# Weight conversion shared over three engines, and TensorE's order left to the planner, in a recurrent attention with a PReLU network behind it

## The chip, the cores and the metric

The kernel runs on one core of a Trainium2 chip. A core has a matrix engine (TensorE, PE in the profile, with its weight loads on a row of their own, PEld), three engines for elementwise work (VectorE or DVE, ScalarE or ACT, GpSimd or POOL), a queue engine that issues DMAs (SyncE or SP; ScalarE can issue DMAs too), and two on-chip memories: SBUF, and PSUM, into which TensorE writes. The engines run their own instructions in order and wait for each other by semaphores. The metric is the device time of one execution in microseconds (us), as the median over several runs. A profile is taken of one execution; its span is the time from the first to the last instruction.

## The reference

Input: q, k, v and f_logit of shape (batch 4, heads 8, sequence 768, head dimension 48) in float32, and a network of 384 to 2048 to 384 whose two weight matrices arrive as float64.

```python
f = 1.0 / (1.0 + np.exp(-f_logit))
for t in range(S):
    state = f[:, :, t, :, None] * state + k[:, :, t] (outer) v[:, :, t]
    y[:, :, t] = q[:, :, t] @ state
x = y, heads side by side: (3072 tokens, 384)
h = x @ w_in
g = np.maximum(h, 0.0) + alpha * np.minimum(h, 0.0)
out = g @ w_out
```

Each head so carries a 48 by 48 state through the sequence that every step decays per row and adds to. The network then treats each token alone.

## The kernel before

The work is cut into twelve chunks: six stretches of 128 tokens of the sequence (c), times two pairs of batch elements (bp). A chunk has 2 x 8 heads and 256 tokens. The order is c outside, bp inside. A chunk's state goes on to the chunk of the next c with the same bp.

For each chunk `attention` loads f, q, k and v. Its preparation is work of VectorE, with GpSimd computing running products of the decay (`pre`, `suf`, L203 to L212): products of q and k with decay factors, in `qd`, `kr`, `us`, `k4`, `q3`, `ks`, `kh` (L173 to L233). TensorE then makes these parts: `raw` (L246) and `qu` (L262) for each of the two batch elements, both copied under masks into `ad` by VectorE (L253, L267); `off` (L280); the transposes `pk` (L288), copied by ScalarE to `ksn`; `pd` (L301), which VectorE adds into the state (L314, L315); and `py` (L336, L347), which is the chunk's output. All of these go through the PSUM tag "pair", which has two buffers. ScalarE copies `py` to `y`, and ten small DMAs turn it into `xT` (L358), the network's input.

`network` works through the 2048 hidden columns in eight groups of two blocks of 128: for each block three matmuls (384 rows in three tiles of 128) with the 256 tokens of xT as moving operand, both blocks into one of four PSUM banks, `ph` (L371). The profile counts 96 such records a chunk. ScalarE takes relu(-h) (L376), VectorE combines it with alpha into `g` (L379; the tag has ten buffers, a chunk uses eight). Then, for each of the two batch elements, the sixteen blocks of g are multiplied with w_out into `po` (L386; 64 records a chunk), which ScalarE copies out (L389).

The weights arrive as float64, of which a float32 has to be made by integer and float operations on the two 32-bit halves: `load_weights` does it in 12 pieces of 512 columns for each matrix, and each piece is seven VectorE operations (L134 to L143). Its raw data uses the tag "y", its temporaries the tag "neg".

Which engine does what is in the code. The order of the instructions on an engine is made by a planner when the program is built: it walks through an expected timeline, and gives each engine the first instruction in the order of the program whose inputs and buffers it expects to be ready. For TensorE alone this is switched off before: inside `tc.manual_schedule` (L406) its instructions stay in the order in which the loop at L407 to L424 calls the generators. `attention` and `network` therefore give up control (`yield`) after each stage; the loop puts two, two, one, two and one groups of the previous chunk's ph behind the five stages of the attention, and the previous network's po after the next chunk's preparation. The weights w_in are asked for after chunk 0's attention, w_out after chunk 1's.

Of the kernel before, what the change touches and what calls it, by code (L numbers as in the profile page):

```python
# [14 lines left out]
C = 128  # L15
# [3 lines left out]
U = 2  # L19
# [7 lines left out]
def kernel(  # L27
# [93 lines left out]
    A = const.tile([128, U, H, C], F32, tag="A", name="A")  # L121
    nc.gpsimd.memset(A, 0.0)

    def load_weights(dst, src, name):

        flat = dst.rearrange("p a n -> p (a n)")
        for n in range(0, flat.shape[1], WP):
            raw = work.tile([128, WP, 2], I32, tag="y", name=f"{name}_raw{n}")
            nc.scalar.dma_start(out=raw.rearrange("p n two -> p (n two)"),
                                in_=src[:, n:n + WP].bitcast(I32))  # L130
            lo, hi = raw[:, :, 0], raw[:, :, 1]

            mi = work.tile([128, WP], I32, tag="neg", name=f"{name}_mi{n}", bufs=3)
            nc.vector.tensor_scalar(mi, hi, 0xFFFFF, 0x100000, ALU.bitwise_and, ALU.bitwise_or)  # L134
            m = mi.bitcast(F32)
            nc.vector.scalar_tensor_tensor(m, lo.bitcast(U32), 2.0 ** -32, mi, ALU.mult, ALU.add)

            e = work.tile([128, WP], I32, tag="neg", name=f"{name}_e{n}", bufs=3)
            nc.vector.tensor_scalar(e, hi, 20, 0x7FF, ALU.logical_shift_right, ALU.bitwise_and)
            nc.vector.tensor_scalar(e, e, 1023.0 - 127.0, 0.0, ALU.subtract, ALU.max)  # L140
            nc.vector.tensor_scalar(e, e, 255.0, 2.0 ** 23, ALU.min, ALU.mult)
            nc.vector.scalar_tensor_tensor(e, hi, -0x80000000, e, ALU.bitwise_and, ALU.bitwise_or)
            nc.vector.scalar_tensor_tensor(flat[:, n:n + WP], m, 2.0 ** -20, e.bitcast(F32), ALU.mult, ALU.mult)  # L143

    def rows(par):
        return slice(64 * par, 64 * par + D)
# [2 lines left out]
        return t.rearrange("p (n r) -> p n r", r=4)  # L149

    def attention(bp, c, state, xT):

        i = f"{bp}_{c}"
        b0 = U * bp

        def load(name, src):
            t = work.tile([128, W], F32, tag=name, name=f"{name}_{i}")
            nc.sync.dma_start(out=t.rearrange("p (u x) -> p u x", u=U),
                              in_=src[b0:b0 + U, c].rearrange("u p h t -> p u (h t)"))
            return t  # L160
# [1 line left out]
        f = quads(load("f", fT))  # L162
        nc.scalar.activation(f, f, AF.Sigmoid)
        qdv = [qd[:, d * W:(d + 1) * W] for d in range(4)]
        nc.sync.dma_start(out=qdv[0].rearrange("p (u x) -> p u x", u=U),
                          in_=qT[b0:b0 + U, c].rearrange("u p h t -> p u (h t)"))
        k = load("k", kT)
        vt = work.tile([128, U, DM + 16], F32, tag="v", name=f"v_{i}")
        nc.gpsimd.memset(vt[:, :, DM:DM + 16], 0.0)
# [29 lines left out]
                fq[:, :, 1:1 + n].unsqueeze(3).broadcast_to((128, G, n, 4)), ALU.mult)  # L199


        suf = work.tile([128, G, NB], F32, tag="suf", name=f"suf_{i}")
        nc.gpsimd.memset(suf, 1.0)  # L203
        pin = pre[:, :, 1:NB + 1]
        nc.gpsimd.tensor_copy(pin, fq)
# [8 lines left out]
            h *= 2  # L214


        q3 = work.tile([128, GC, 3, DB], F32, tag="q3", name=f"q3_{i}")
        ks = work.tile([128, GC, 2, DB], F32, tag="ks", name=f"ks_{i}")
        kh = work.tile([128, GC, DB], F32, tag="kh", name=f"kh_{i}")
        for j in range(2):  # L220
            js = slice(j, G, 2)
            nc.vector.tensor_tensor(q3[:, :, 2 * j].rearrange("p g (i r) -> p g i r", r=4), q4[:, js],
# [9 lines left out]
        nc.vector.tensor_tensor(f64.rearrange("p u h c -> p (u h c)").unsqueeze(2),  # L232
                                f32[:, 0:G:2], f32[:, 1:G:2], ALU.mult)  # L233
        qs = q3.rearrange("p (u h c) s t -> p u h c (s t)", h=HP, c=NC2)

        yield


        for u in range(U):
            raw = pair(f"raw{u}_{i}")  # L240
            for hp in range(HP):
                for j in range(NJ):
                    g = (u * HP + hp) * C + j * DB
                    for par in range(2):
                        r_ = rows(par)
                        nc.tensor.matmul(raw[DB * j:DB * (j + 1), par, hp * C:(hp + 1) * C],  # L246
                                         lhsT=k[r_, g:g + DB],
                                         rhs=qd[r_, 0:4 * W].rearrange("p (d x) -> p d x", d=4)[:, :, g:g + DB],
                                         start=True, stop=True)
            adu = ad[:, u].rearrange("p r h t -> p (r h) t")  # L250
            rv = raw.rearrange("p r (h d t) -> p (r h) d t", h=HP, d=4)
            for d in range(4):
                nc.vector.copy_predicated(  # L253
                    adu, mraw[:, d].rearrange("p i r -> p (i r)").bitcast(I32).unsqueeze(1).broadcast_to((128, H, DB)),
                    rv[:, :, d])
            qu = pair(f"qu{u}_{i}")
            for hp in range(HP):
                for j in range(NJ):
                    g = (u * HP + hp) * NJ + j
                    for par in range(2):  # L260
                        r_ = rows(par)
                        nc.tensor.matmul(qu[DB * j:DB * (j + 1), par, hp * UW:(hp + 1) * UW],  # L262
                                         lhsT=k4[r_, g * DB:(g + 1) * DB], rhs=us[r_, g], start=True, stop=True)
            for m in range(1, NB):
                lo = UO[m] + (4 if m == 1 else 0)
                n = DB - 4 * m
                nc.vector.copy_predicated(  # L267
                    ad[:, u, :, :, 4 * m:DB],
                    mquad[:, lo:lo + n].bitcast(I32).unsqueeze(1).unsqueeze(1).broadcast_to((128, 2, HP, n)),
                    qu[:, :, 0:HP * UW].rearrange("p r (h x) -> p r h x", h=HP)[:, :, :, lo:lo + n])  # L270
            yield
        off = pair(f"off_{i}")
        for u in range(U):
            for hp in range(HP):
# [14 lines left out]
        ksn = work.tile([128, U, HP * 128], F32, tag="ksn", name=f"ksn_{i}", bufs=1)  # L289
        for u in range(U):  # L290
            nc.scalar.copy(ksn[:, u], pk[:, u])
        yield
        pd = pair(f"pd_{i}")
        for u in range(U):
            for hp in range(HP):
                for cc in range(NC2):
                    for par in range(2):
# [3 lines left out]
                        nc.tensor.matmul(pd[64 * par:64 * par + 64, cc, o:o + D],  # L301
                                         lhsT=ksn[s_, u, hp * 128 + 64 * par:hp * 128 + 64 * par + 64],
                                         rhs=vt[s_, u, hd * D:(hd + 1) * D], start=True, stop=True)
        states = [state[bp]]
        for cc in range(NC2):
            if c == NC - 1 and cc == NC2 - 1:
                break
            st = work.tile([128, U * HP, D], F32, tag="state", name=f"state{cc}_{i}", bufs=6)
            pdv = pd[:, cc, 0:U * HP * D].rearrange("p (a e) -> p a e", e=D)
            if states[-1] is None:  # L310
                nc.vector.tensor_copy(st, pdv)
            else:
                fv = f64[:, :, :, cc:cc + 1].rearrange("p u h o -> p (u h) o")
                nc.vector.tensor_tensor(st, states[-1], fv.broadcast_to((128, U * HP, D)), ALU.mult)  # L314
                nc.vector.tensor_tensor(st, st, pdv, ALU.add)  # L315
            states.append(st)
        state[bp] = states[-1]
        yield


        for j in range(NJ):
# [17 lines left out]
        for cc in range(NC2):  # L339
            if states[cc] is None:  # L340
                continue
            for u in range(U):
                for hp in range(HP):
                    for par in range(2):
# [2 lines left out]
                        nc.tensor.matmul(py[64 * par:64 * par + D, u, o:o + CH],  # L347
                                         lhsT=states[cc][r_, u * HP + hp], rhs=qs[r_, u, hp, cc, 0:CH],
                                         start=False, stop=True, skip_group_check=True)
        y = work.tile([128, U, HP, C], F32, tag="y", name=f"y_{i}")  # L350
        for u in range(U):
            nc.scalar.copy(y[:, u].rearrange("p h t -> p (h t)"), py[:, u])
        for hd in range(H):
            d = hd * D
            while d < (hd + 1) * D:
                n = min((hd + 1) * D, (d // 128 + 1) * 128) - d
                p0 = 64 * (hd % 2) + d - hd * D
                nc.sync.dma_start(  # L358
                    out=xT[d % 128:d % 128 + n, d // 128].rearrange("p (u t) -> p u t", u=U),
                    in_=y[p0:p0 + n, :, hd // 2])  # L360
                d += n
        yield

    def network(bp, c, xT):
        i = f"{bp}_{c}"
        gs = []
        for f in range(0, NF, 2):
# [11 lines left out]
                nc.vector.scalar_tensor_tensor(g[:, j], neg[:, j], om[:, f + j:f + j + 1], phv[:, j],  # L379
                                               ALU.mult, ALU.add)  # L380
            gs.append(g)
            yield
        for u in range(U):
            po = bank(f"po{u}_{i}")
            for f in range(NF):
                nc.tensor.matmul(po[:, 0:DM], lhsT=gs[f // 2][:, f % 2, u * C:(u + 1) * C], rhs=w_out_sb[:, f],  # L386
                                 start=(f == 0), stop=(f == NF - 1))
            o = work.tile([128, DM], F32, tag="o", name=f"o{u}_{i}", bufs=3)
            nc.scalar.copy(o, po[:, 0:DM])  # L389
            t0 = ((U * bp + u) * NC + c) * C  # L390
            nc.sync.dma_start(out=out[t0:t0 + C], in_=o)
        yield

    steps = [(bp, c) for c in range(NC) for bp in range(B // U)]
    state = [None] * (B // U)

    def begin(n):
        x = work.tile([128, NK, T], F32, tag="xT", name=f"xT_{n}")  # L400
        a = attention(*steps[n], state, x)
        next(a)
        return a, x

    att = net = None
    with tc.manual_schedule(engines={mybir.EngineType.PE}):  # L406
        for n in range(len(steps) + 1):  # L407
            if n == 0:
                att, x = begin(n)
            for stage in range(5):  # L410
                if n < len(steps):
                    next(att)
                for _ in range((2, 2, 1, 2, 1)[stage]):
                    if net is not None:
                        next(net)
            if n < 2:
                load_weights((w_in_sb, w_out_sb)[n], (w_in, w_out)[n], ("w_in", "w_out")[n])
            if n < len(steps):
                last = network(*steps[n], x)
            if n + 1 < len(steps):  # L420
                att, x = begin(n + 1)
            if net is not None:
                next(net)
            net = last  # L424


# [53 lines left out]
```

## Time and profile before

| | |
|---|---|
| Runs | 781.1, 782.22 and 784.5 us; median 782.22 |
| The profiled execution | 781.1 us, span 779.2 us |
| TensorE busy | 658.2 us (84% of the span) |
| VectorE busy | 435.6 us (56%) |
| ScalarE busy | 159.1 us (20%) |
| GpSimd busy | 70.6 us (9%) |
| DMA traffic | 46.79 MB, mean 60 GB/s |
| Mean granted TensorE clock | 0.936 |

Busy time counts instructions in execution; the rest of the span an engine waits. A line "L371 PE MATMUL ph<-xT,w_in_sb" names the source line, the engine, the operation, what is written and what is read. Behind it stand the count, the busy time, the mean of one in ns, and the idle time just before these instructions with what ended it. The tenths are the busy share in each of 40 equal slices of the span. Not all idle time costs something: only that of the engine which sets the end at that moment.

### The profile page before, as it was taken

How to read it: one execution, taken by the hardware profiler on the slowest of the kernel's cores; microseconds unless marked ns; L12 is line 12 of the kernel's file. 1: busy time of each engine (PE TensorE's matmuls, PEld its weight loads, DVE VectorE, ACT ScalarE, POOL GpSimd, SP SyncE). 2: the span in 40 equal slices, each digit the busy share in tenths (PEclk: the TensorE clock that was granted, in tenths of full speed). 3: DMA queues.
4: the chain of work that ended last, by engine and by line, in shares of the span. 5: the costliest groups of instructions: out<-in, count | busy, mean ns of one | idle time of the engine just before them, and what ended most of it. 6: DMA issues, size and time to landing. Idle time of an engine off the chain costs nothing.

```text
span 779.2 us, 17567 instructions
## 1 busy us (share of the span) xinstructions
PE 658.2 (84%) x7712; PEld 485.5 (62%) x7712; DVE 435.6 (56%) x920; ACT 159.1 (20%) x289; POOL 70.6 (9%) x228
## 2 busy tenths in 40 slices
PE   0350186468999999899999999999999999999998
PEld 0350175124876777777867857768778678587684
DVE  5798997892861842933916808618439157052030
ACT  2030023000330411410411403204104114041110
POOL 8212002000020020020020100200200200000000
PEclk9995589557999999999999999999999999999999
DMA  4224432440220210211212202202101110000000
GB/s 177 83 84 122 159 105 76 135 145 26 69 67 21 84 42 22 83 41 28 80 48 66 56 24 70 65 22 83 41 23 55 51 40 8 24 13 22 21 0 21
DMA packets 31468, 46.79 MB, mean 60 GB/s; under 512 B 3744, under 2 KB 19104, under 8 KB 31392
## 3 DMA queue, kind: packets, MB, share of 16 engines
q1 hardware_dynamic: 27648, 33.04, 14.2%
q10 hardware_dynamic: 3744, 12.63, 5.1%
q8 instruction: 61, 1.00, 0.5%
q14 instruction: 15, 0.12, 0.1%
HBM read 36.22 MB, written 4.72 MB: 53 GB/s over the span
## 4 chain that ended last, share of the span: by engine, by line
PE 67%; DVE 21%; DMA 5%; POOL 3%; ACT 1%; issue 1%; SPq 1%; ACTq 0%; DVEq 0%; POOLq 0%
PE po L386 31%; PE ph L371 24%; PE py L336 3%; DVE qd L182 3%; PE py L347 3%; DVE g L379 2%; DVE ad L267 2%; PE raw L246 2%; DMA qd<-in_qT 2%; DVE ad L253 2%; PE pd L301 2%; PE pk L288 2%; PE qu L262 1%; DMA w_in_raw<-in_w_in 1%; DMA w_out_raw<-in_w_out 1%; DVE k L191 1%
## 5 line engine op out<-in xcount | busy, mean ns | idle before, releaser
L371 PE MATMUL ph<-xT,w_in_sb 128*128 128x256 f32 x1152 | 269.2, 390 | 37.5 <-DVE w_in_sb L143 37.5
L386 PE MATMUL po<-w_out_sb,g 128*128 128x384 f32 x768 | 264.5, 504 | 29.3 <-DVE w_out_sb L143 29.3
L371 PEld LDWEIGHTS ph<-xT,w_in_sb 128*128 128x128 f32 x1152 | 218.4, 194 | 73.0 <-DVE w_in_sb L143 39.2
L386 PEld LDWEIGHTS po<-w_out_sb,g 128*128 128x128 f32 x768 | 149.0, 196 | 140.5 <-DVE w_out_sb L143 32.9
L253 DVE COPY_PREDICATED ad<-mraw,raw 128x256 f32<-128x256 int32 x96 | 42.7, 444 | 174.6 <-PE raw L246 172.4
L379 DVE SCALAR_TENSOR_TENSOR g<-neg,om,ph 128x256 f32<-128x256 f32 x192 | 84.3, 475 | 72.5 <-ACT neg L376 72.2
L376 ACT ACTIVATE neg<-ph 128x512 f32<-128x512 f32 x96 | 57.3, 597 | 201.6 <-PE ph L371 131.8
L389 ACT COPY o<-po 128x384 f32<-128x384 f32 x24 | 11.5, 478 | 278.5 <-PE po L386 278.5
L267 DVE COPY_PREDICATED ad<-mquad,qu 128x224 f32<-128x224 int32 (+6 forms) x168 | 49.7, 296 | 5.2 <-DVE ad L253 0.5
L246 PE MATMUL raw<-qd,k 48*32 48x128 f32 x1536 | 29.4, 286 | 19.4 <-DVE qd L182 19.4
L196 DVE TENSOR_TENSOR us<-us,fq 128x768 f32<-128x768 f32 (+2 forms) x72 | 44.3, 615 | 0.0
L203 POOL MEMSET suf<- 128x256 f32 x12 | 3.7, 311 | 418.4 <-DVE ks L225 418.4
L246 PEld LDWEIGHTS raw<-qd,k 48*32 48x32 f32 x1536 | 22.8, 110 | 28.5 <-POOL pre L212 19.4
L262 PE MATMUL qu<-us,k 48*32 48x116 f32 x1536 | 27.3, 273 | 12.4 <-DVE us L196 6.9
L323 ACT COPY A<-ad 32x512 f32<-32x512 f32 x48 | 29.6, 617 | 20.1 <-DVE ad L267 19.7
L262 PEld LDWEIGHTS qu<-us,k 48*32 48x32 f32 x1536 | 22.5, 109 | 13.7 <-DVE us L196 7.3
L232 DVE TENSOR_TENSOR f<-pre 128x16 f32<-128x16 f32 x12 | 2.2, 184 | 47.8 <-POOL pre L212 47.7
L210 POOL TENSOR_TENSOR suf<-suf,pre 128x32 f32<-128x32 f32 (+2 forms) x84 | 28.8, 368 | 1.8
L182 DVE TENSOR_TENSOR qd<-qd,f 128x768 f32<-128x768 f32 (+2 forms) x36 | 27.5, 764 | 1.9 <-DMA qd<-in_qT 1.8
L336 PE MATMUL py<-A,v 128*64 128x128 f32 x384 | 24.9, 285 | 2.5 <-DVE us L196 2.5
L288 PE MATMUL pk<-ident,ks 128*128 128x128 f32 x96 | 13.9, 291 | 14.5 <-DVE ad L267 11.7
L336 PEld LDWEIGHTS py<-A,v 128*64 128x64 f32 x384 | 22.0, 143 | 6.3 <-issue 6.3
(60 smaller groups left out, 429.8 us busy)
## 6 DMA issues: line engine op xcount, KB each, us to landing
f<-in_fT SPq DMA_DIRECT2D x12, 512.0 KB, 3.7
k<-in_kT SPq DMA_DIRECT2D x12, 512.0 KB, 5.5
qd<-in_qT SPq DMA_DIRECT2D x12, 512.0 KB, 4.0
w_in_raw<-in_w_in ACTq DMA_DIRECT2D x12, 512.0 KB, 3.5
w_out_raw<-in_w_out ACTq DMA_DIRECT2D x12, 512.0 KB, 3.5
v<-in_v SPq DMA_DIRECT2D x12, 384.0 KB, 3.3
out<-o SPq DMA_DIRECT2D x24, 192.0 KB, 1.9
xT<-y SPq DMA_DIRECT2D x72, 48.0 KB, 2.0
```

What stands on the lines that cost most here:

```text
L182: nc.vector.tensor_tensor(quads(qdv[d])[:, :, d:4], quads(qdv[d - 1])[:, :, d:4], f[:, :, 1:5 - d], ALU.mult)
L196: nc.vector.tensor_tensor(us[:, :, UO[m]:UO[m] + 4 * n].rearrange("p g (i r) -> p g i r", r=4), us[:, :, skip:skip + 4 * n].rearrange("p g ...
L246: nc.tensor.matmul(raw[DB * j:DB * (j + 1), par, hp * C:(hp + 1) * C], lhsT=k[r_, g:g + DB], rhs=qd[r_, 0:4 * W].rearrange("p (d x) -> p d ...
L253: nc.vector.copy_predicated(adu, mraw[:, d].rearrange("p i r -> p (i r)").bitcast(I32).unsqueeze(1).broadcast_to((128, H, DB)), rv[:, :, d])
L262: nc.tensor.matmul(qu[DB * j:DB * (j + 1), par, hp * UW:(hp + 1) * UW], lhsT=k4[r_, g * DB:(g + 1) * DB], rhs=us[r_, g], start=True, stop= ...
L267: nc.vector.copy_predicated(ad[:, u, :, :, 4 * m:DB], mquad[:, lo:lo + n].bitcast(I32).unsqueeze(1).unsqueeze(1).broadcast_to((128, 2, HP, ...
L323: nc.scalar.copy(A[s_, :, :, s_], ad[s_].rearrange("p u r h t -> p u (r h) t"))
L336: nc.tensor.matmul(py[64 * par:64 * par + 64, u, hp * C:(hp + 1) * C], lhsT=vt[:, u, hd * D:hd * D + 64], rhs=A[:, u, par * HP + hp], star ...
L371: nc.tensor.matmul(ph[:, j * T:(j + 1) * T], lhsT=w_in_sb[:, kt, (f + j) * 128:(f + j + 1) * 128], rhs=xT[:, kt], start=(kt == 0), stop=(k ...
L376: nc.scalar.activation(neg, phv, AF.Relu, scale=-1.0)
L379: nc.vector.scalar_tensor_tensor(g[:, j], neg[:, j], om[:, f + j:f + j + 1], phv[:, j], ALU.mult, ALU.add)
L386: nc.tensor.matmul(po[:, 0:DM], lhsT=gs[f // 2][:, f % 2, u * C:(u + 1) * C], rhs=w_out_sb[:, f], start=(f == 0), stop=(f == NF - 1))
```

## The change

The conversion of a piece has four VectorE operations in place of seven; two steps are done by ScalarE (`activation` with Relu, which scales and shifts the exponent field and cuts it off at zero, and with Copy, which scales the mantissa) and the last product by GpSimd. The raw tiles have a tag of their own with four buffers and are loaded by SP's queue; the temporaries use the tag "g". The pieces of w_in come in the order in which the network's tiles need them: for each block of 512 columns, the three row blocks.

TensorE's order is no longer fixed: `manual_schedule`, the generators and the loop with stages are gone. A plain loop calls the attention of a chunk, the weights' load in the first two, and then the network of the chunk before, and the planner orders TensorE's instructions like those of the other engines.

To make room, several tags go from two buffers to one (`suf`, `q3`, `ks`, `kh`, `y`), the state's from six to five, `o` from three to two. q is loaded into a tile of its own and copied by ScalarE to `qd`, instead of by DMA straight to `qd`. The ten DMAs from y to xT are split between the queues of SP and ScalarE.

```diff
+    bias = const.tile([128, 1], F32, tag="bias", name="bias")
+    nc.gpsimd.memset(bias, -896.0 * 2.0 ** 23)
...
-        for n in range(0, flat.shape[1], WP):
-            raw = work.tile([128, WP, 2], I32, tag="y", name=f"{name}_raw{n}")
-            nc.scalar.dma_start(out=raw.rearrange("p n two -> p (n two)"),
-                                in_=src[:, n:n + WP].bitcast(I32))
+        ks = NK if dst is w_in_sb else 1
+        per = flat.shape[1] // ks
+        for n in [k * per + j for j in range(0, per, WP) for k in range(ks)]:
+            raw = work.tile([128, WP, 2], I32, tag="raw", name=f"{name}_raw{n}", bufs=4)
+            nc.sync.dma_start(out=raw.rearrange("p n two -> p (n two)"),
+                              in_=src[:, n:n + WP].bitcast(I32))
             lo, hi = raw[:, :, 0], raw[:, :, 1]
 
-            mi = work.tile([128, WP], I32, tag="neg", name=f"{name}_mi{n}", bufs=3)
+            e = work.tile([128, WP], I32, tag="g", name=f"{name}_e{n}", bufs=10)
+            nc.vector.tensor_scalar(e, hi, 0x7FF00000, None, ALU.bitwise_and)
+            nc.scalar.activation(e, e, AF.Relu, bias=bias, scale=8.0)
+
+            mi = work.tile([128, WP], I32, tag="g", name=f"{name}_mi{n}", bufs=10)
             nc.vector.tensor_scalar(mi, hi, 0xFFFFF, 0x100000, ALU.bitwise_and, ALU.bitwise_or)
             m = mi.bitcast(F32)
-            nc.vector.scalar_tensor_tensor(m, lo.bitcast(U32), 2.0 ** -32, mi, ALU.mult, ALU.add)
-
-            e = work.tile([128, WP], I32, tag="neg", name=f"{name}_e{n}", bufs=3)
-            nc.vector.tensor_scalar(e, hi, 20, 0x7FF, ALU.logical_shift_right, ALU.bitwise_and)
-            nc.vector.tensor_scalar(e, e, 1023.0 - 127.0, 0.0, ALU.subtract, ALU.max)
-            nc.vector.tensor_scalar(e, e, 255.0, 2.0 ** 23, ALU.min, ALU.mult)
+            nc.scalar.activation(m, mi, AF.Copy, scale=2.0 ** -20)
+            nc.vector.scalar_tensor_tensor(m, lo.bitcast(U32), 2.0 ** -52, m, ALU.mult, ALU.add)
             nc.vector.scalar_tensor_tensor(e, hi, -0x80000000, e, ALU.bitwise_and, ALU.bitwise_or)
-            nc.vector.scalar_tensor_tensor(flat[:, n:n + WP], m, 2.0 ** -20, e.bitcast(F32), ALU.mult, ALU.mult)
+            nc.gpsimd.tensor_tensor(flat[:, n:n + WP], m, e.bitcast(F32), ALU.mult)
...
-        nc.sync.dma_start(out=qdv[0].rearrange("p (u x) -> p u x", u=U),
-                          in_=qT[b0:b0 + U, c].rearrange("u p h t -> p u (h t)"))
+        q = load("q", qT, 1)
+        nc.scalar.copy(qdv[0], q)
...
-                nc.sync.dma_start(
+                (nc.sync if hd % 2 else nc.scalar).dma_start(
...
-    with tc.manual_schedule(engines={mybir.EngineType.PE}):
-        for n in range(len(steps) + 1):
-            if n == 0:
-                att, x = begin(n)
-            for stage in range(5):
-                if n < len(steps):
-                    next(att)
-                for _ in range((2, 2, 1, 2, 1)[stage]):
-                    if net is not None:
-                        next(net)
-            if n < 2:
-                load_weights((w_in_sb, w_out_sb)[n], (w_in, w_out)[n], ("w_in", "w_out")[n])
...
+    for c in range(NC):
+        for bp in range(B // U):
+            xT = work.tile([128, NK, T], F32, tag="xT", name=f"xT_{bp}_{c}")
+            state[bp] = attention(bp, c, state[bp], xT)
+            if c == 0:
+                load_weights((w_in_sb, w_out_sb)[bp], (w_in, w_out)[bp], ("w_in", "w_out")[bp])
+            if todo is not None:
+                network(*todo)
+            todo = (bp, c, xT)
+    network(*todo)
```

More of the change, by code (lines that the diff above doesn't have):

```diff
@@ L154, in attention, with load @@
         b0 = U * bp
-        def load(name, src):
-            t = work.tile([128, W], F32, tag=name, name=f"{name}_{i}")
+        def load(name, src, bufs=2):
+            t = work.tile([128, W], F32, tag=name, name=f"{name}_{i}", bufs=bufs)
             nc.sync.dma_start(out=t.rearrange("p (u x) -> p u x", u=U),
@@ L199, in attention @@
                 fq[:, :, 1:1 + n].unsqueeze(3).broadcast_to((128, G, n, 4)), ALU.mult)
-        suf = work.tile([128, G, NB], F32, tag="suf", name=f"suf_{i}")
+        suf = work.tile([128, G, NB], F32, tag="suf", name=f"suf_{i}", bufs=1)
         nc.gpsimd.memset(suf, 1.0)
@@ L214, in attention @@
             h *= 2
-        q3 = work.tile([128, GC, 3, DB], F32, tag="q3", name=f"q3_{i}")
-        ks = work.tile([128, GC, 2, DB], F32, tag="ks", name=f"ks_{i}")
-        kh = work.tile([128, GC, DB], F32, tag="kh", name=f"kh_{i}")
+        q3 = work.tile([128, GC, 3, DB], F32, tag="q3", name=f"q3_{i}", bufs=1)
+        ks = work.tile([128, GC, 2, DB], F32, tag="ks", name=f"ks_{i}", bufs=1)
+        kh = work.tile([128, GC, DB], F32, tag="kh", name=f"kh_{i}", bufs=1)
         for j in range(2):
@@ L234, in attention @@
         qs = q3.rearrange("p (u h c) s t -> p u h c (s t)", h=HP, c=NC2)
-        yield
         for u in range(U):
@@ L270, in attention @@
                     qu[:, :, 0:HP * UW].rearrange("p r (h x) -> p r h x", h=HP)[:, :, :, lo:lo + n])
-            yield
         off = pair(f"off_{i}")
@@ L291, in attention @@
             nc.scalar.copy(ksn[:, u], pk[:, u])
-        yield
         pd = pair(f"pd_{i}")
@@ L303, in attention @@
                                          rhs=vt[s_, u, hd * D:(hd + 1) * D], start=True, stop=True)
-        states = [state[bp]]
+        states = [state]
         for cc in range(NC2):
@@ L307, in attention @@
                 break
-            st = work.tile([128, U * HP, D], F32, tag="state", name=f"state{cc}_{i}", bufs=6)
+            st = work.tile([128, U * HP, D], F32, tag="state", name=f"state{cc}_{i}", bufs=5)
             pdv = pd[:, cc, 0:U * HP * D].rearrange("p (a e) -> p a e", e=D)
@@ L316, in attention @@
             states.append(st)
-        state[bp] = states[-1]
-        yield
         for j in range(NJ):
@@ L349, in attention @@
                                          start=False, stop=True, skip_group_check=True)
-        y = work.tile([128, U, HP, C], F32, tag="y", name=f"y_{i}")
+        y = work.tile([128, U, HP, C], F32, tag="y", name=f"y_{i}", bufs=1)
         for u in range(U):
@@ L361, in attention @@
                 d += n
-        yield
+        return states[-1]
     def network(bp, c, xT):
@@ L381, in network @@
             gs.append(g)
-            yield
         for u in range(U):
@@ L387, in network @@
                                  start=(f == 0), stop=(f == NF - 1))
-            o = work.tile([128, DM], F32, tag="o", name=f"o{u}_{i}", bufs=3)
+            o = work.tile([128, DM], F32, tag="o", name=f"o{u}_{i}")
             nc.scalar.copy(o, po[:, 0:DM])
@@ L391, in network @@
             nc.sync.dma_start(out=out[t0:t0 + C], in_=o)
-        yield
-    steps = [(bp, c) for c in range(NC) for bp in range(B // U)]
+    todo = None
     state = [None] * (B // U)
[L399 to L405, printed above, removed]
-    with tc.manual_schedule(engines={mybir.EngineType.PE}):
-        for n in range(len(steps) + 1):
-            if n == 0:
-                att, x = begin(n)
-            for stage in range(5):
-                if n < len(steps):
-                    next(att)
-                for _ in range((2, 2, 1, 2, 1)[stage]):
-                    if net is not None:
-                        next(net)
-            if n < 2:
-                load_weights((w_in_sb, w_out_sb)[n], (w_in, w_out)[n], ("w_in", "w_out")[n])
[L418 to L424, printed above, removed]
+    for c in range(NC):
[8 more added lines that the diff above has]
+    network(*todo)
 def _level_masks():
```

## The prediction

> **What bounds the kernel now.** I read the page's busy shares and slices first, then a table of stretches, then the groups, the chain of waits and the timeline.
>
> The page, busy share and then tenths in 40 slices of 19.5 us:
>
> ```profile
> PE 658.2 (84%) x7712; PEld 485.5 (62%) x7712; DVE 435.6 (56%) x920; ACT 159.1 (20%) x289; POOL 70.6 (9%) x228
> ...
> PE   0350186468999999899999999999999999999998
> ...
> DVE  5798997892861842933916808618439157052030
> ```
>
> TensorE is full from the eleventh slice on and half empty before; VectorE is the reverse. Two kernels in one: a start of some 185 us that VectorE sets, and the rest, which TensorE sets. The stretches say how sharply (columns: length, then busy us and instructions of PE, PEld, DVE, ACT, POOL, then granted clock, DMA share, GB/s):
>
> ```profile
> 60.00:80.00 20.00, 1.22 (x2) 0.50 (x2) 16.77 (x39) 0.00 (x0) 3.03 (x6) 0.50 0.45 138
> 80.00:100.00 20.00, 5.60 (x13) 4.06 (x14) 19.45 (x40) 0.00 (x0) 0.00 (x0) 0.51 0.46 139
> ...
> 160.00:180.00 20.00, 12.40 (x16) 4.29 (x16) 19.35 (x40) 0.00 (x0) 0.00 (x0) 0.50 0.41 129
> ...
> 400.00:450.00 50.00, 48.95 (x639) 37.30 (x638) 28.43 (x61) 13.13 (x24) 4.80 (x17) 1.00 0.19 54
> ```
>
> At 60 to 100 and 140 to 180 us VectorE does conversion and ScalarE nothing; PE has two to sixteen matmuls in 20 us, at half clock. The waits name the cause, and the only one that recurs later (total, times, longest):
>
> ```profile
> PE ph L371 <- DVE w_in_sb L143: 37.5, 3, 17.2
> ...
> PE po L386 <- DVE w_out_sb L143: 29.3, 12, 9.0
> ...
> PE pk L288 <- DVE ad L267: 11.7, 9, 2.4
> ```
>
> The steady part, from the chain in order of time: po groups begin at 338.95, 392.62, 446.27, 500.07, so a chunk takes 53.7. Its pure TensorE work: the last network, alone, 20.72 (ph) + 20.66 (po) = 41.4; attention by start-to-start times at 302.9 to 336.1: raw and qu 2 x 1.9, off 0.8, pk 1.0, pd 1.1, py 3.8 = 10.5. Sum 51.9, so TensorE waits 1.8 a chunk. From 185.05, where PE runs without gaps, the span closes as: rest of the first po 9.5 + ten chunks 537 + 3 (one chunk was 56.6) + last network 41.4 + 3.3 after PE's end = 594; 185 + 594 = 779.
>
> **What the Trainium skill says.** "TensorE: Matmul & The Clock Gate", section "What's actually happening": an idle TensorE is gated to half its clock. The trace agrees: 0.50 in the conversion stretches, 1.00 once full, so every gap closed also speeds what follows it. "SBUF — State Buffer", "Who interferes with whom": a VectorE operation with two SBUF inputs, or in its two-port mode, and a GpSimd operation that reads SBUF exclude each other. The trace agrees in part:
>
> ```profile
> 12.98 2.30 POOL L210 TENSOR_TENSOR suf<-suf,pre 128x32 f32<-128x32 f32 x4
> ...
> 336.98 1.09 POOL L210 TENSOR_TENSOR suf<-suf,pre 128x32 f32<-128x32 f32 x4
> ```
>
> The same four operations take 2.30 beside a working VectorE and 1.09 beside an idle one, while VectorE's L182 grew only from 0.96 to 1.15.
>
> **The change, part by part.** The rows used:
>
> ```profile
> L136 DVE SCALAR_TENSOR_TENSOR w_out_mi<-w_out_raw,w_out_mi 128x512 f32<-128x512 uint32 x12 | 8.2, 685 | 0.0
> ...
> L139 DVE TENSOR_SCALAR w_out_e<-w_out_raw 128x512 int32<-128x512 int32 x12 | 5.1, 422 | 0.0
> ...
> L376 ACT ACTIVATE neg<-ph 128x512 f32<-128x512 f32 x96 | 57.3, 597 | 201.6 <-PE ph L371 131.8 <-DVE w_in_sb L143 48.3 <-issue 19.3
> ```
>
> *VectorE.* A piece now has four TENSOR_SCALAR at about 0.43 and three SCALAR_TENSOR_TENSOR at 0.69: 3.78, 24 pieces 90.7. After: 2 x 0.43 + 2 x 0.69 = 2.24, 53.7. Saved 37.0, all on the engine that sets the start.
>
> *GpSimd* gets one 128x512 product a piece. Not in the trace. L210 and L212 take 0.27 at 32 columns and 0.45 at 128, 1.85 ns a column, so 1.16 us; the skill's "GPSIMD Engine Reference", "3.1 Elementwise — side-by-side cycle accounting", has 2.6 cycles per element, 4497 ns at 2048, a quarter of which is 1.12. 24 x 1.16 = 28 us beside some 110 us: GpSimd has room. What it takes from VectorE through the shared port lies between 0 and 28; I take 10, since in the trace GpSimd bore most of the wait.
>
> *ScalarE* gets two operations a piece from SBUF: L163 takes 1.06 at 1024, so about 0.63 at 512, and the skill's "ScalarE: Activation LUTs", "What ACT_TABLE_LOAD costs", adds 93 ns for the bias column: 24 x 1.35 = 32, and the q copy 12 x 1.06 = 13. ScalarE is 20% busy and idle in the conversion stretches: nothing, if pieces overlap. Without that cover a piece is a relay of VectorE, ScalarE, VectorE and GpSimd of some 5 us; with four raw buffers, up to five pairs of g buffers and attention work to fill in, the relay is hidden.
>
> *Loads.* Weights move from ScalarE's queue, where the first waited until 53.45 for the y buffer, to SP with four buffers of their own, so they can start at once: 12.6 MB at q10's rate (12.63 MB in 5.1% of 779 = 40 us) is hidden under VectorE. Each of 24 issues waits, with the raw buffer, for VectorE's last use; behind it on SP stand loads of f, q, k, v and half the xT stores, late by up to one piece, 2.2, covered by VectorE's queue in the start. Ten xT stores a chunk took 6.4 on SP; split over two queues about 3, and the others cost ScalarE some 3 us of issue a chunk. Covered later by network matmuls; uncovered 2 to 3 a chunk. The q buffer lets q load early and replaces DMA waits by a 1.06 copy.
>
> *Single buffers* for suf, q3, ks, kh, y: the six operations at L222 to L230 (6 x 0.68 = 4.1) must wait until the previous chunk's off, pk or py is done. The 20 us of po matmuls hide that; uncovered 4.1 a chunk.
>
> *Order of pieces.* The first network can start after 3 pieces of w_in instead of 9. Now its first ph groups stalled till 95.6; afterwards they can run from when xT lands, about 57.
>
> *End of the start.* VectorE's work before the last w_out piece: attention (435.6 - 90.7 conversion - 84.3 at L379 - 2.8 for om) / 12 = 21.5 a chunk. Two chunks 43.0 + conversion 53.7 + half a network's L379 3.5 + port 10 = 110.2. At 90% busy (93% in 40 to 120 us now, less for the relay) 122, from 9.3 on: 132 instead of 181. The third chunk's preparation, some 16 us of VectorE work that now stands ahead of w_out, comes after it in program order.
>
> *TensorE's order.* Without the fixed order the planner places PE's instructions as it does the other engines': the first in the program among those it expects to be ready. That is attention n ahead of network n-1, which fills its holes. How good are its expectations? In the timeline VectorE's order, which it made, puts 2.5 us of other work between the state sum at 328.65, which follows pd, and the g pair at 331.19, which follows twelve ph matmuls (2.6 us) and a 0.6 activation; more ready work was at hand (L229) and was put behind. So it expected about the real PE time. It expected GpSimd faster than it is: VectorE waited 4.76 at L232, ahead of a g that was ready. So PE's order should be usable, but each of some eight hand-offs a chunk (raw, qu, raw, qu, off, pk, pd, py) is placed as soon as expected. I take 0.3 late at each, 2.4 a chunk, for today's 1.8, of which pk's wait (11.7 over nine) may go: 2.5. Bounds: 1, and 7.
>
> *Sum.* At 132, PE has left: half the first ph 10.4, its po 20.7, ten chunks at 51.9 + 2.5 = 544, last network 41.4, tail 3.3: 620. Span 752. The profiled execution took 781.1 for a span of 779.2; with those 1.9, 754, and the median of the runs lies 1.1 above that execution: **755 us**, against 782.22.
>
> **The rivals.**
> 1. *Slower: the fixed order was worth more than the start.* Place: attention's hand-offs in the ten full chunks. At 0.9 late each, 7.0 a chunk: 132 + 595 + 70 = 797, run 800. It decides from 5.2 a chunk. For: a chunk's slack above PE's work is only 1.8, bought by 5 us of ph matmuls placed by hand at every hand-off, and GpSimd is misjudged. Against: 20 us of po matmuls are free to fill.
> 2. *Port-bound conversion:* the whole 28 lands on VectorE, 18 more at 90%: end of the start 152, run 775. For: nearly all conversion operations read two inputs or use two ports. Against: L182's small growth.
> 3. *Better:* no port loss, the relay full, 1.8 a chunk: (100.2 / 0.97) + 9.3 = 113; 113 + 594 + 3 = 730 by run.
> 4. *It doesn't do what it says:* the planner holds the first network behind attention until VectorE is through, and start and order cancel: 782. For: L379 stands after w_out in program order. Against: VectorE's 37 us alone move the end of w_out's conversion forward.
>
> **How the numbers follow.** Likeliest 0.50, own range 738 to 768; better 0.12; port-bound 0.10; cancelled 0.05; slower 0.23. Some 0.5% is about what a measurement of this kernel can tell from no change. Faster 0.72, same 0.05, slower 0.23. The range, 728 to 802, leaves about 0.05 below and 0.12 above.
>
> **What would show it.** Right: in the slices VectorE full and PE low until about 130 us, then full; conversion groups at 2 x 0.43 and 2 x 0.69 on VectorE; GpSimd's products at 1.2 to 2; po groups 54 to 55 apart. Wrong: VectorE idle in the start behind ScalarE, GpSimd or a raw load (relay or port); PE waits of several us a chunk on L253, L267 or L323's line (rival 1), or raw matmuls split up among ph, which would lengthen the attention's 10.5.

## The result, and the profile after

The changed kernel takes 792.93 us (792.04 to 793.55, four runs) against 782.67 for the kernel before: ratio 1.0129, 95% interval 1.0104 to 1.0155. It is slower by 1.3%, where 755 us and faster was forecast. The profiled execution has a span of 790.0 us.

The page after, busy share and tenths in 40 slices (19.75 us each):

```profile
PE 660.0 (84%) x7712; PEld 490.1 (62%) x7712; DVE 413.5 (52%) x848; ACT 199.3 (25%) x349; POOL 124.1 (16%) x253
...
PE   0255551999989998989989989989989979989998
...
DVE  6799897937257257167076076086085094043030
```

TensorE is full three slices earlier than before, as forecast, but then has an 8 in every third slice where it had nines. The table of stretches (length, then PE, PEld, DVE, ACT, POOL busy us and instructions, clock, DMA share, GB/s) gives both ends:

```profile
120.00:140.00 20.00, 5.21 (x72) 4.18 (x73) 14.28 (x26) 6.66 (x11) 17.44 (x19) 0.50 0.21 64
140.00:160.00 20.00, 20.00 (x77) 14.38 (x76) 16.97 (x34) 3.81 (x6) 4.28 (x13) 1.00 0.09 27
...
400.00:450.00 50.00, 45.69 (x573) 34.69 (x557) 28.90 (x63) 13.66 (x24) 4.82 (x17) 1.00 0.18 57
```

In the steady part PE has 45.7 busy us in 50, before 48.95, both at a granted clock of 1.00: what is lost there is time in which TensorE stands, not clock. The chain in order of time (start, length, what) shows the same as a period, before:

```profile
181.17 13.71 PE po L386 x36
...
446.27 20.64 PE po L386 x64
...
500.07 20.64 PE po L386 x64
```

and after:

```profile
148.95 20.64 PE po L386 x64
...
204.68 20.64 PE po L386 x64
...
320.52 20.64 PE po L386 x64
...
378.40 20.64 PE po L386 x64
```

From one chunk's po to the next it is 57.9 us, before 53.7. The two effects work against each other. The first network's po ends at 169.6 instead of 194.9: 25 us gained. From there to the end the ten chunks cost 36 us more. The difference is the 11 us between the spans.

Where the steady 57.9 goes is in the timeline of one chunk (start, length, engine, line, what; in brackets the idle time before it and what ended it):

```profile
341.98 1.07 PE L267 MATMUL qu<-us,k 48*32 48x116 f32 x64
342.30 1.89 DVE L258 COPY_PREDICATED ad<-mraw,raw 128x256 f32<-128x256 int32 x4 [20.19 <-PE raw L251]
...
344.33 1.15 PE L251 MATMUL raw<-qd,k 48*32 48x128 f32 x64 [1.28 <-DVE ad L258]
...
345.41 0.70 PE L372 MATMUL ph<-xT,w_in_sb 128*128 128x256 f32 x2
...
346.76 1.08 PE L267 MATMUL qu<-us,k 48*32 48x116 f32 x64 [0.66 <-DVE ad L272]
...
349.73 0.75 PE L284 MATMUL off<-q,kh 48*32 48x32 f32 x64 [0.39 <-DVE ad L258]
...
355.43 1.15 PE L304 MATMUL pd<-v,ksn 64*64 64x48 f32 x64 [1.20 <-ACT ksn L295]
...
359.56 1.97 PE L337 MATMUL py<-A,v 128*64 128x128 f32 x32 [0.62 <-ACT A L324]
```

The second raw stands right behind the first qu. It needs the PSUM buffer that VectorE's four masked copies are still reading, and TensorE waits 1.28 us. Before, 24 ph matmuls (5.4 us) stood there:

```profile
303.77 1.08 PE L262 MATMUL qu<-us,k 48*32 48x116 f32 x64
...
304.78 5.45 PE L371 MATMUL ph<-xT,w_in_sb 128*128 128x256 f32 x24
...
310.15 1.16 PE L246 MATMUL raw<-qd,k 48*32 48x128 f32 x64
```

Now two ph records, then six, six, six and ten stand between the attention's groups, and 66 behind them, where the only wait is 0.27. With that 0.27 the waits of this chunk are 4.4 us. The rest of the 5.9 above the 51.9 of pure work is in the changes between the attention's small matmuls and ph: two ph records take 0.70 where they take 0.43 in a row, and the seven stretches of ph of this chunk come to 1.5 more than 96 records in a row. The ends of matmuls are modelled in the profile, so the split between wait and change is less sure than their sum.

### The profile page after: what moved, and what is told of

Read it like the earlier page. It is cut to its first block, busy times and chain, and to the rows that moved or that the text cites. A ratio compares the mean times of both kernels' runs of the same rounds, so it can differ in the third digit from the quotient of the medians.

```text
span 790.0 us, 17642 instructions
## 1 busy us (share of the span) xinstructions
PE 660.0 (84%) x7712; PEld 490.1 (62%) x7712; DVE 413.5 (52%) x848; ACT 199.3 (25%) x349; POOL 124.1 (16%) x253
## 4 chain that ended last, share of the span: by engine, by line
PE 49%; DVE 29%; POOL 8%; ACT 5%; DMA 4%; issue 3%; ACTq 1%; SPq 0%; POOLq 0%; DVEq 0%
PE po L386 31%; PE ph L372 14%; DVE ad L258 5%; DVE ad L272 4%; DMA f<-in_fT 3%; POOL suf L217 3%; POOL pre L219 3%; ACT A L324 3%; DVE us L194 2%; POOL pre L212 2%; DVE g L380 2%; DVE qd L189 2%; DVE q L229 2%; DVE us L203 1%; PE py L337 1%
## 5 line engine op out<-in xcount | busy, mean ns | idle before, releaser
L386 PE MATMUL po<-w_out_sb,g 128*128 128x384 f32 x768 | 249.6, 486 | 0.0
L372 PEld LDWEIGHTS ph<-xT,w_in_sb 128*128 128x128 f32 x1152 | 216.7, 193 | 52.6 <-issue 22.4
L386 PEld LDWEIGHTS po<-w_out_sb,g 128*128 128x128 f32 x768 | 145.9, 190 | 99.2
L380 DVE SCALAR_TENSOR_TENSOR g<-neg,om,ph 128x256 f32<-128x256 f32 x192 | 81.8, 475 | 97.1 <-ACT neg L377 91.2
L251 PE MATMUL raw<-qd,k 48*32 48x128 f32 x1536 | 31.8, 302 | 50.5 <-DVE qd L189 35.4
L251 PEld LDWEIGHTS raw<-qd,k 48*32 48x32 f32 x1536 | 24.7, 116 | 58.9 <-issue 37.9
L176 POOL MEMSET v<- 128x32 f32 x12 | 1.8, 148 | 368.3 <-PE py L337 368.3
L267 PE MATMUL qu<-us,k 48*32 48x116 f32 x1536 | 29.2, 285 | 30.5 <-DVE ad L272 13.4
L328 ACT COPY A<-off 32x256 f32<-32x256 f32 x48 | 15.1, 360 | 47.0 <-PE off L284 46.8
L219 POOL TENSOR_TENSOR pre<-pre 128x32 f32<-128x32 f32 (+2 forms) x84 | 26.5, 342 | 0.9
```

The costliest lines, as they stand in the source:

```text
L372: nc.tensor.matmul(ph[:, j * T:(j + 1) * T], lhsT=w_in_sb[:, kt, (f + j) * 128:(f + j + 1) * 128], rhs=xT[:, kt], start=(kt == 0), stop=(k ...
```

## Experiments

Theory H: the loss is TensorE's order, with the attention's groups placed one close behind the other. Its rivals: the planner as such; the single buffers, q copy and stores that lengthen the attention's own chain; a conversion that gained nothing. "Period" below is the time from one chunk's po to the next, as most settled chunks have it; single chunks are up to 3.8 us longer. Ratios are to runs of the kernel before made beside each run (medians 782.4 to 783.2).

### The order put back, in two ways

`conv_fixed` is the changed kernel with the stages, the loop and the fixed order of before. `conv_staged` has the stages and the loop, but not the fixed order, so its diff is the same without the `manual_schedule` line. The loop over `n` is that of before, and so are the places of the `yield`s:

```diff
-    todo = None
...
+    steps = [(bp, c) for c in range(NC) for bp in range(B // U)]
...
+    with tc.manual_schedule(engines={mybir.EngineType.PE}):
+        for n in range(len(steps) + 1):
...
```

> The changed kernel, with TensorE's order of before put back (stages, loop and fixed order); conversion, loads, single buffers, q copy and split xT stores stay as changed. Theory H (the loss is TensorE's order: attention groups placed one behind the other, with too few ph matmuls between them, 5.9 us of waits and switches a chunk in place of 1.8): po groups again about 53.7 apart, the earlier end of the start kept, so 782.7 - 25 = about 757 us (750 to 765). Rival S (the single buffers, the q copy and the stores on ScalarE make the attention's own chain longer): 57 to 58 apart in this order too, 790 to 800 us.

> As conv_fixed, with the stages and the loop that sets ph groups behind them in the program, but TensorE left to the planner. Theory H1 (what costs is the plain loop's order of calls, which the planner takes as priority): the steady order is nearly the fixed one, period 53.5 to 54.5, 750 to 765 us. Rival H2 (the planner's expectations themselves are too short, so any order of its own loses): period above 56, 775 us or more.

Measured: `conv_staged` 759.5 us, ratio to before 0.9693 (0.9665 to 0.9721), period mostly 55.2. `conv_fixed` 801.82 us, ratio 1.0233 (1.0198 to 1.0268), period 55.6 to 57.3. H1 gets the time right, with the period 0.7 above its range; for `conv_fixed` I had expected 757 and missed by 45.

More than half of that miss is in the start: the second po begins at 230.7, where 25 us ahead of the 227.9 of before would be 203. The rest is the period; all of TensorE's waits from 250 to 650 us are at pk (20.9 us). TensorE's waits over the whole run in `conv_fixed` (total, times, longest):

```profile
PE pk L295 <- DVE ad L274: 30.5, 10, 3.7
PE po L393 <- POOL w_out_sb L151: 30.4, 12, 8.9
```

and the timeline of TensorE there (columns as above):

```profile
152.14 1.65 PE L393 MATMUL po<-w_out_sb,g 128*128 128x384 f32 x2 [2.98 <-POOL w_out_sb L151]
156.03 2.93 PE L393 MATMUL po<-w_out_sb,g 128*128 128x384 f32 x4 [2.24 <-POOL w_out_sb L151]
159.92 1.65 PE L393 MATMUL po<-w_out_sb,g 128*128 128x384 f32 x2 [0.96 <-POOL w_out_sb L151]
```

A piece of w_out arrives every 3.89 us: the relay of VectorE, ScalarE, VectorE and GpSimd runs one piece at a time. VectorE's first operation of a piece waits for GpSimd's product (in the changed kernel this line has no wait):

```profile
L142 DVE TENSOR_SCALAR w_out_e<-w_out_raw 128x512 int32<-128x512 int32 x12 | 5.1, 427 | 15.1 <-POOL w_out_sb L151 15.1
```

In the fixed order all of the first network's ph precedes po, so when w_out is converted its eight g tiles can hold eight of the tag's ten buffers; a piece needs two. That this is the reason is read from the code; the wait above agrees with it, but no run with more buffers was made. The prediction had named "up to five pairs of g buffers" as the relay's cover; here the cover was gone, and the seven VectorE operations of before, at 3.8, would have been no slower. The first po ends at 194.1, in the kernel before at 194.9.

### Each part alone

`before_plain` is the kernel before with only the plain loop (no stages, no fixed order). `order_only` is the kernel before with its stages and loop, and TensorE left to the planner (the `manual_schedule` line taken out). `planner_old_conv` is the changed kernel with the old conversion (its seven VectorE operations, and its loads on ScalarE's queue):

```diff
-        for n in [k * per + j for j in range(0, per, WP) for k in range(ks)]:
+        for n in range(0, flat.shape[1], WP):
...
```

> The kernel before with the plain loop of the changed kernel and TensorE left to the planner; conversion, loads, buffers and q as before. The one part alone. Theory H1 (the plain loop costs what the steady part loses): po groups 57 to 58 apart, 10 x 3.8 more than before, less what the planner gains in the start (order_only: 19 us): 798 to 812 us. Rival (single buffers, q copy and stores are needed for the loss): 54 to 55 apart, below 775 us.

> The kernel before with the planner ordering TensorE too, the staged loop kept; nothing else changed. Theory H1 (what costs in the changed kernel is the plain loop's order of calls, not the planner): po groups 53.5 to 54.5 apart as in before (54.0), and the start a little shorter, since PE no longer stands behind a ph that waits for weights: 765 to 780 us. Rival H2 (the planner loses by itself): over 56 apart, 795 or more.

> The changed kernel with the seven-operation conversion of before (loads on ScalarE's queue, matrices in row order, raw tiles in their own tag with four buffers); plain loop and planner stay. Theory H: period 57.8 as in the changed kernel, and the start ends later by the conversion's worth, 793 + 25 = 812 to 825 us. Rival C (the conversion gained little, the earlier end of the start came from the plain loop's order): 793 to 800 us.

| kernel | us | ratio to before (interval) | period | second network's po begins at |
|---|---|---|---|---|
| before | 782.7 | 1 | 53.7 | 227.9 |
| order_only | 763.55 | 0.9767 (0.9733 to 0.9802) | 53.7 | 212.5 |
| before_plain | 829.36 | 1.0599 (1.0556 to 1.0642) | 57.1 | 240.8 |
| planner_old_conv | 809.15 | 1.033 (1.0299 to 1.0362) | 57.8 | 222.9 |
| changed | 792.93 | 1.0129 (1.0104 to 1.0155) | 57.9 | 204.7 |
| conv_staged | 759.5 | 0.9693 (0.9665 to 0.9721) | 55.2 | 194.4 |

In the staged program the planner is acquitted: it keeps the period at 53.7 and begins sooner, since TensorE stands for less time at ph and po that lack their weights (35.5 us instead of 66.8 over the whole run). With the plain loop as well the period is 57.1 and the kernel 6% slower than before, more than the 798 to 812 I had expected, because its start got longer too: one qu waited 28.9 us, until 184.5, for the end of w_out's conversion on VectorE. The plain loop in a fixed order was not run. The new conversion with its loads and order of pieces is worth 16 us with the same plain loop (809.15 to 792.93; theory H had put it at 19 or more), all ahead of the second po (222.9 to 204.7).

### The product on GpSimd

```diff
-            nc.gpsimd.tensor_tensor(flat[:, n:n + WP], m, e.bitcast(F32), ALU.mult)
+            nc.vector.tensor_tensor(flat[:, n:n + WP], m, e.bitcast(F32), ALU.mult)
```

> The changed kernel with the last product of a piece on VectorE in place of GpSimd (five VectorE operations). Theory P (GpSimd's product costs VectorE through the shared port about what it saves: conversion took 71.8 us of VectorE time instead of 53.7): each of the four other operations back to 0.43 and 0.69, conversion 53.7 + 24 x 0.69 = 70 us, time the same within 4 us (789 to 797). Rival (the stretch is not GpSimd's doing): conversion 88 us on VectorE, the start longer by 15 to 20, 808 or more.

Measured: 789.93 us, ratio to before 1.0084 (1.0053 to 1.0115). Groups of w_out in the changed kernel (count, busy us, mean ns of one, idle before):

```profile
L151 POOL TENSOR_TENSOR w_out_sb<-w_out_mi,w_out_e 128x512 f32<-128x512 f32 x12 | 18.2, 1537 | 16.7 <-DVE w_out_mi L149 15.2 <-DVE w_out_e L150 1.5
...
L149 DVE SCALAR_TENSOR_TENSOR w_out_mi<-w_out_raw,w_out_mi 128x512 f32<-128x512 uint32 x12 | 10.2, 861 | 0.0
```

and in this one:

```profile
L149 DVE SCALAR_TENSOR_TENSOR w_out_mi<-w_out_raw,w_out_mi 128x512 f32<-128x512 uint32 x12 | 8.2, 686 | 0.6 <-ACT w_out_mi L148 0.6
...
L151 DVE TENSOR_TENSOR w_out_sb<-w_out_mi,w_out_e 128x512 f32<-128x512 f32 x12 | 8.2, 686 | 0.0
```

With the product on GpSimd the four VectorE operations of all pieces took 71.8 us, where the durations of before come to 53.7; with the product on VectorE all five took 72, of which the same four 55.7. So the move saved VectorE 16 us and cost it 16. The Trainium skill's "SBUF — State Buffer", "Who interferes with whom", has a VectorE operation with two SBUF inputs and a GpSimd operation that reads SBUF exclude each other. The trace agrees: L149, which reads two, takes 861 ns beside the GpSimd product and 686 without it. That the port is the reason is the page's account; the runs show the exchange.

### Why 55.2 and not 53.7: the early q

`staged_qdma` is `conv_staged` with q loaded straight into qd again; `plain_qdma` is the changed kernel with the same edit.

```diff
-        q = load("q", qT, 1)
-        nc.scalar.copy(qdv[0], q)
+        nc.sync.dma_start(out=qdv[0].rearrange("p (u x) -> p u x", u=U),
+                          in_=qT[b0:b0 + U, c].rearrange("u p h t -> p u (h t)"))
```

> conv_staged with q loaded by DMA straight into qd, as before, in place of the tile of its own and ScalarE's copy. Theory Q (the early q lets VectorE take up the next chunk's us product of 2.0 us between this chunk's masked copies, and pk waits for the last of these, 2.3 us a chunk in place of 1.3): the wait at pk back to about 1.3, period from 55.2 to 54.0 to 54.4, 748 to 753 us. Rival B (the single buffers or the xT stores on ScalarE make the difference of 1.2 a chunk): period stays 55.2, 757 to 762 us.

> The changed kernel with q loaded by DMA straight into qd. Theory Q: the masked copies end about 2 us earlier here too; period from 57.8 to about 56.5, 778 to 783 us. Rival (in the plain loop other hand-offs set the pace): 57.8, 791 to 795 us.

Measured: `staged_qdma` 743.55 us, ratio to before 0.9508 (0.9491 to 0.9526), period 53.6 once settled; `plain_qdma` 792.83 us, ratio 1.014 (1.0108 to 1.0172), period 57.1 to 57.9 with two of over 61. VectorE in `conv_staged`:

```profile
449.14 0.40 DVE L274 COPY_PREDICATED ad<-mquad,qu 128x224 f32<-128x224 int32 x1
...
450.00 0.35 DVE L274 COPY_PREDICATED ad<-mquad,qu 128x192 f32<-128x192 int32 x1
450.27 1.98 DVE L194 TENSOR_TENSOR us<-qd,f 128x1024 f32<-128x1024 f32 x1
...
452.17 0.32 DVE L274 COPY_PREDICATED ad<-mquad,qu 128x160 f32<-128x160 int32 x1
...
455.20 0.18 DVE L274 COPY_PREDICATED ad<-mquad,qu 128x32 f32<-128x32 int32 x1
...
455.53 1.06 PE L295 MATMUL pk<-ident,ks 128*128 128x128 f32 x8 [2.36 <-DVE ad L274]
```

The next chunk's us product, 2 us, has slipped in between two of this chunk's copies, because q was there early; pk waits for the last copy. With the DMA, whose data comes later, the us product stands behind the last copy (446.27 after 446.16 in the chunk of `staged_qdma` at about the same time), and TensorE's waits at pk fall from 20.8 to 11.0 us over the whole run. In these two chunks the time from the start of off to the start of pk is 3.74 us with the copy and 1.79 with the DMA; two ph records, 0.43 in a row, stand in the first, so 1.5 of the 1.6 a chunk lie there. So a load made earlier delayed what mattered. In the plain loop theory Q fails: there other hand-offs set the pace (from 250 to 650 us TensorE waits 8.9 us at raw, 8.3 at off and 3.7 at qu, and at pk never for a masked copy), and the edit changes nothing.

### How much ph behind each hand-off

The groups set behind the five stages were 2, 2, 1, 2, 1. `staged_23111` changes this in `conv_staged`, `staged_11114` and `staged_23210` in `staged_qdma`. The edit of the last:

```diff
-                for _ in range((2, 2, 1, 2, 1)[stage]):
+                for _ in range((2, 3, 2, 1, 0)[stage]):
```

> conv_staged with three ph groups in place of two behind the second raw and qu, and one in place of two behind pd. Theory Q: the wait at pk (2.3 us a chunk) is covered by 2.7 us more of ph, nothing else waits: period 53 to 53.5, 738 to 748 us. Rival: the wait moves on to pd or py, which have less ph ahead of them: period 54.5 or more, 752 to 760 us.

> staged_qdma with one ph group in place of two behind the raw and qu stages (1, 1, 1, 1, then 4). Theory S (what the staged order buys is slack behind each hand-off; the planner expects too soon by up to 1.3 us, so one group of 2.6 us is enough for the raw stages, while pk and py see their inputs later): raw again without a wait, pd, pk and py with 1 to 2 us together; period 54.5 to 56, 752 to 768 us. Rival (only the place in the program matters, not how much stands there): period 53.6 to 54, 742 to 748 us.

> staged_qdma with the groups set 2, 3, 2, 1, 0: more cover ahead of pk and pd, none behind py. Theory S: pk's wait (1.2 a chunk) goes, pd keeps its cover, py gets one group less: period 52.5 to 53.2, 732 to 741 us. Rival (py waits for ScalarE's copies into A instead): period 54 or more, 745 us or more.

| groups | q | us | ratio to before (interval) | period | waits of PE from 250 to 650 us |
|---|---|---|---|---|---|
| 2 3 1 1 1 | copy | 758.8 | 0.9699 (0.9684 to 0.9714) | 54.6 to 56.9, one 58.3 | pd 14.9, pk 2.6 |
| 1 1 1 1 4 | DMA | 759.56 | 0.9704 (0.9682 to 0.9726) | 54.6 to 54.9, one 57.8 | pd 10.0, pk 2.6 |
| 2 2 1 2 1 | DMA | 743.55 | 0.9508 (0.9491 to 0.9526) | 53.6 | pk 8.4 |
| 2 3 2 1 0 | DMA | 731.06 | 0.934 (0.9323 to 0.9357) | 52.6 | none |

`staged_23111` moved the wait from pk to pd, which is its rival's case: one group stands between the two, as in `conv_staged`, and ScalarE copies ksn, for which pd waits, behind the next chunk's sigmoid and copies into A (from 456.74 to 461.05 in one chunk). With one group at each place the raw stages don't wait either, as theory S had it, but pd does. With 2, 3, 2, 1, 0 no wait is left in this stretch, and the page's slices show it:

```profile
PE   0145796779999999999999999999999999999998
```

The period of 52.6 is 0.7 above the 51.9 worked out ahead as pure work. With 731.06 us the kernel beats both, and lies just below theory S's 732 to 741.

### The product on VectorE in the staged order

`staged_qdma_pdve` is `staged_qdma` with the product on VectorE.

> staged_qdma with the last product of a piece on VectorE. Theory P (GpSimd's product costs VectorE through the port what it saves): conversion again 72 us of VectorE, TensorE's wait for w_out_sb (18.1) no longer behind a GpSimd operation of 1.5 to 1.8 us but of 0.69: 737 to 744 us. Rival: VectorE's fifth operation lengthens the start, 750 or more.

Measured: 737.12 us, ratio to before 0.9421 (0.9405 to 0.9436), some 6 us less than `staged_qdma`. TensorE's wait for w_out_sb fell from 18.1 to 8.0. Together with the groups 2, 3, 2, 1, 0 it was not run.

## Why the prediction was wrong, point by point

*The bound and its split* held: the sum of start and ten periods accounts for both spans. The forecast span was 752; the 38 us missing are 6.5 in the start (po from 149.0, forecast 132 + 10.4 = 142.4) and 32 in ten chunks (57.6 on average from 169.6 to 745.3, forecast 54.4).

*VectorE's saving* of 37.0: the count of operations was right, the durations were not. The conversion's four operations took 18 more than their durations of before, where I had put 10, inside the range of 0 to 28; 16 of the 18 went when the product left GpSimd. GpSimd's product took 1.54 and 1.87 on average where I had worked out 1.16; ScalarE's two operations took 0.62, and 0.72 with the bias column, as forecast. The relay was hidden in the changed kernel, and not in `conv_fixed`. TensorE's run began at 136.75 with half of the ph to do, as forecast, 4.75 later.

*TensorE's order* is the step that failed. "I take 0.3 late at each, 2.4 a chunk ... 2.5" was 4.4 of waits and 1.5 of changes between matmul kinds: 5.9, above the 5.2 from which the first rival was said to decide. That rival (7.0 a chunk, 800 us) is the case that came, with its place right and its price 1.1 too high. Two things were wrong in the step. I tested the planner's expectations at ph and g, where they were good, and not at the masked copies, behind which the second raw waited 1.28 us a chunk. (What the planner expected is not on record; that it took the copies for done is inferred from the place it gave to this raw.) And I reasoned that "20 us of po matmuls are free to fill": the planner fills a hole only if it expects one, and in the plain loop the attention comes ahead of all ph and po of the chunk before. I named the program's order as the planner's priority and did not draw the conclusion: what the change lost was not the fixed order but the slack that the staged loop wrote into the program. `order_only` and `before_plain` show it. The changes between matmul kinds stood at nothing in the sum of 51.9. They were there before too: I read the 1.8 a chunk above that sum as waits, but the waits at pk are 10.6 us over eight chunks from 250 to 650 us, 1.3 each.

*Single buffers:* `staged_23210` runs with all of them and, from 250 to 650 us, no wait: they cost nothing in that order. The early q with its copy, which I had as a gain or nothing, cost 1.6 a chunk in the staged order (55.2 to 53.6).

*The chances:* 0.72 for faster rested on the planner step above all; that step's bounds of 1 and 7 held the measured 5.9, and I put too little weight on the upper one.

## What to carry to other kernels

A planner that picks the first ready instruction packed a chain of short hand-offs, where the program put them first, more tightly than they went, and TensorE waited; put filler between the hand-offs in the order of the program, by how long each takes on the slower engine, and read from the waits where a group is short. Judge "fixed order" and "order of the program" apart: here leaving TensorE to the planner gained 2.3% with the staged program, and with the plain loop the same kernel was 6% slower than before. Before moving an operation off the bounding engine or a load forward, ask what the receiver shares with that engine, and which less urgent work the earlier data lets in.

## What the runs showed that was not expected

A GpSimd product of 128x512 took 1.54 to 1.87 us on average beside a working VectorE, and stretched VectorE's own operations of 0.43 and 0.69 to 0.43 to 0.98 and 0.79 to 0.95; moving it off VectorE saved no VectorE time. Where VectorE waited for it, for w_out in `conv_fixed`, it took 1.26. A handful of ph matmuls between small attention matmuls costs 0.15 to 0.28 us more than the same number in a row, as the profile has it. With the tags' buffers short, the conversion over three engines went at 3.89 us a piece, as slow as seven VectorE operations.
